# Background work of a fused attention kernel: due steps for the feed-forward products, and two slots a step for one half of the mixing

## The chip, the cores and the metric

The kernel runs on one core of one Trainium2 chip. Its time is the device time of one execution in microseconds (us), the median of 3 runs. The engines are named as the profile names them: PE is the matrix engine, PEld its weight loads, DVE the vector engine, ACT the scalar engine, POOL the GpSimd engine, SP the engine that issues the transfers.

## The reference

Three layers follow each other, all in float32, for 4 batches of 576 positions and a model width of 512:

```python
scores = np.where(causal, -1e9, scale * q @ k.T + np.minimum(bias, 0.0))   # attention, 8 heads of 64
attn = softmax(scores) @ v
h = xt @ U @ V                                   # mixing over positions, rank 32
u = x + h.transpose(0, 2, 1)
x = u + np.maximum(u @ w_ch1, 0.0) @ w_ch2       # feed-forward, 512 -> 2048 -> 512
out = moe2(x)                                    # 4 single-head causal attentions, the top 2 gated and summed
```

## The kernel before

The program has three stages: the first attention, the rest of the feed-forward, and the second attention. Every float32 product that must be exact is split: an operand is held as a rounded high part and a low part, and one product becomes three (high by high, high by low, low by high). The change touches the first stage alone.

**The first attention.** `Attn.run` (L449) walks over steps. A step computes one tile of the scores of one head (`qk`, L361 and L362, PE), its mask and maximum (`peak`, L372, DVE), and the exponential of the tile before (L379, ACT). Ten steps later (`LAG`) the tile is transposed (`t`, L402 and L405, PE) and copied out of PSUM into `pt` (L85 on ACT, L87 on DVE). There are 5 tiles a head, 2 heads a pair, 4 pairs a batch and 4 batches: 160 steps with scores and some 12 more in which the last tiles drain. So ten steps make a pair, and each step has one `qk` tile, by which steps can be counted in the trace. Every tenth step or so the products with V (`pv`, L429, PE) of a finished pair run, and `pv_done` (L791) copies them into `uT` on ACT (L85).

At the end of every step `fillers(i)` (L913) issues what else the step carries: the operands of coming pairs (`prep_steps`, with DMAs on SP's queue), one or two pieces of the conversion of the weights (`CONVS`, two a step in steps 41 to 69), and as many calls of `background()` (L867) as `BG = (1, 1, 0, 2, 1)` has for the step modulo 5. Everything is issued in the order in which this Python code runs, and each engine works through its own share in that order.

**Background work.** Two queues feed `background()`.

- `mixq` holds the mixing of one batch in two halves (`mix_tasks`, L224). A half is ten tasks: three `rows` (transposes `mx` on PE, then `xh` on ACT and `xl` on DVE), an empty one, `down` (ten products `mt` on PE, then `tt` on ACT and DVE), an empty one, and four `up` (two products `mo` on PE each, then an addition into `uT` on DVE). Half one is queued by `pv_done` of a batch's second pair, half two by that of its fourth. The `up` tasks of half two also split the input of the first feed-forward chunk (`u_split`, L272: `uh` on ACT, `ul` on DVE or POOL); two more tasks follow, the last of which fills the other queue.
- `ffnq` holds the feed-forward of the batch over the first three of the sixteen weight blocks (`ffn_tasks`, L280), for two chunks of 288 positions: per chunk three `first` tasks (twelve products `hps` on PE, then `hh` on ACT and `hl` on DVE) and four `second` tasks (nine products `facc` on PE, then an addition into `stage` on DVE). 14 tasks a batch, for batches 0 to 2. A task whose weights aren't converted yet has to wait; the third block is whole from step 73 on.

The tasks of half two from the first `up` on but the last `KD + 2` may not start while `ffnq` holds anything. `background()` as it was alternates between the queues by a counter, `turn`, as long as both have something that may run. PSUM banks for all these (`bank`, L809) come from the pool of four that the score tiles use, but for one step in ten.

Two more things are issued by step number: `halves` at steps 152, 154, 156 and 158 (weights of the next stage), and `ufirst` at steps 161 to 164, which first empties `ffnq` and then splits the first input of the next stage.

Of the kernel before, what the change touches and what calls it, by code (L numbers as in the profile page):

```python
# [20 lines left out]
DM, DFF, E, R = 512, 2048, 4, 32  # L21
P = 128
NP = H // 2
NT = 5
KD = DM // P
# [27 lines left out]
STREAM = (((0, 0), (3, -3)), ((-1, 4),), ((0, 1),), ((0, 2), (1, -2)), ((1, -1),), ((0, 3),))  # L53
FAST = (40, 70)
RAWS = 4

ENGA = ('vaaaaa', 'aavaav')
ULA = ("vvvv", "gvgg")
# [13 lines left out]
BG = (1, 1, 0, 2, 1)  # L72
# [10 lines left out]
def cp(nc, eng, out, in_):  # L83
    if eng == "a":
        nc.scalar.activation(out=out, in_=in_, func=AF.Copy)  # L85
    else:
        nc.vector.tensor_copy(out=out, in_=in_)  # L87
# [57 lines left out]
def f32_stream(jobs, order):  # L145

    n = len(jobs)
    for i in range(-3, n + 1):
        for pieces in order:
            l = [jobs[i + d][3][x] if x >= 0 else jobs[i + d][x + 3] for d, x in pieces if 0 <= i + d < n]  # L150
            if l:
                def step(l=l):
                    for f in l:
                        f()
                yield step
# [3 lines left out]
def fused_kernel(ctx, tc, qk, v, s, u, vv, w12, wp, out):  # L159
# [17 lines left out]
    full = {}  # L177

    def wjobs(f, width, cpool, wpool, room, fixed={}, raws=2, wide=1):


        def job(c0):
            x, c = divmod(c0, DM)

            def load(raw):
                nc.sync.dma_start(out=raw, in_=w12[f, :, x, c:c + width])

            if f in Wf:
                return f32_stages(nc, cpool, room, load, P, width, f"w{f}_{c0}",
                                  dest=lambda: Wf[f][:, x, c:c + width], fixed=fixed, raws=raws, wide=wide)  # L190

            def use(t):
                if c0 == 0:
                    Wh[f] = wpool().tile([P, 2, DM], F32R, tag="wh", name=f"wh_{f}")
                    Wl[f] = wpool().tile([P, 2, DM], F32R, tag="wl", name=f"wl_{f}")
                wh, wl = Wh[f][:, x, c:c + width], Wl[f][:, x, c:c + width]
                nc.scalar.activation(out=wh, in_=t, func=AF.Copy)  # L197
                yield
                eng = nc.vector if WLE == "v" else nc.gpsimd
                eng.tensor_tensor(out=wl, in0=t, in1=wh.bitcast(F32), op=OP.subtract)  # L200
                full[f] = full.get(f, 0) + width

            return f32_stages(nc, cpool, room, load, P, width, f"w{f}_{c0}", use, fixed=fixed, raws=raws, wide=wide)

        return [job(c0) for c0 in range(0, 2 * DM, width)]
# [478 lines left out]
    with ExitStack() as cx:  # L684
# [5 lines left out]
        NPR = B * NP  # L690
# [8 lines left out]
        def load_v(p):  # L699
            b, pr = divmod(p, NP)  # L700
            Vs[p] = d2.tile([P, NT, P], F32, tag="V", name=f"V_{p}")
            nc.sync.dma_start(out=Vs[p], in_=v[b, pr])
# [88 lines left out]
        def pv_done(p, ps, half=None):  # L791
            b, pr = divmod(p, NP)
            if half is None:
                cp(nc, "a", uT[:, pr, b * S:b * S + S].rearrange("p (a b) -> p a b", a=2), ps)
            else:
                cp(nc, "a", uT[:, pr, b * S + HALF * half:b * S + HALF * half + HALF], ps)
            if half == 0:
                return
            if pr == 1:
                mixes[b] = mix_tasks(b, bank)  # L800
                mixq.extend((f, False) for f in mixes[b][0])
            if pr == NP - 1 and b < B - 1:
                first, then = ffn_a(b)
                m = mixes[b][1]
                for k in range(KD):
                    m[k - KD] = lambda f=m[k - KD], g=first[k]: (f(), g())
                mixq.extend((f, x >= len(m) - KD) for x, f in enumerate(m + [lambda: None, lambda: ffnq.extend(then)]))

        def bank(name):  # L809
            if now[0] in WIDE:  # L810
                return psq.tile([P, 2, 512], F32, tag="qk2", name=name, bufs=1)[:, 0, :]
            return psq.tile([P, 1, 512], F32, tag="qk1", name=name, bufs=4)[:, 0, :]

        now = [0]

        def ffn_a(b):


            def done(c, d, ps):
                if d == 0:  # L820
                    stage["t"] = d2.tile([P, KD, CH], F32, tag="stage", name=f"stage_{c}", bufs=1)
                nc.vector.tensor_tensor(out=stage["t"][:, d, :], in0=ps, in1=uT[:, d, c * CH:c * CH + CH], op=OP.add)
                if d == KD - 1:
                    nc.sync.dma_start(out=aD[:, :, c * CH:c * CH + CH], in_=stage["t"])

            return ffn_tasks(range(FA), [2 * b, 2 * b + 1], d2, bank, done)

        mixq, ffnq, stage, mixes = [], [], {}, {}
# [16 lines left out]
        def use_v(t, x):  # L845
            cs = slice(THIRD * x, THIRD * x + THIRD)
            nc.scalar.activation(out=V4[:, 0, cs], in_=t, func=AF.Copy)
            yield
            nc.vector.tensor_tensor(out=V4[:, 1, cs], in0=t, in1=V4[:, 0, cs].bitcast(F32), op=OP.subtract)

        def job(load, n, name, use):
            return f32_stages(nc, cv, PIECE, load, P, n, name, use, fixed=fixed, raws=RAWS, wide=2)

        jobs = [job(lambda raw: nc.sync.dma_start(out=raw, in_=u), NT * R, "u", use_u)]
        for x in range(S // THIRD):
            jobs.append(job(lambda raw, x=x: nc.sync.dma_start(out=raw, in_=vv[x]), THIRD, f"v{x}",
                            lambda t, x=x: use_v(t, x)))
        jobs += [j for f in range(FA + GROUPS[0]) for j in wjobs(f, PIECE, cv, lambda: w01p, PIECE, fixed, RAWS, 2)]
        convs = list(f32_stream(jobs, STREAM))
# [7 lines left out]
        def background():  # L867


            turn[0] += 1  # L870
            ffn = ffnq and full.get(ffnq[0][0]) == 2 * DM
            if mixq and (turn[0] % 2 or not ffn) and not (mixq[0][1] and ffnq):
                mixq.pop(0)[0]()
            elif ffn:
                ffnq.pop(0)[1]()

        def halves(i):

# [4 lines left out]
            nc.scalar.activation(out=Wh[f][:, x], in_=Wf[f][:, x], func=AF.Copy)  # L883
            nc.vector.tensor_tensor(out=Wl[f][:, x], in0=Wf[f][:, x], in1=Wh[f][:, x].bitcast(F32), op=OP.subtract)

        turn = [0]
        todo = {}
        for i in range(2 * GROUPS[0]):
            todo.setdefault(HALVES + 2 * i, []).append(lambda i=i: halves(i))
# [22 lines left out]

        def fillers(i):  # L913
            p, r = divmod(i, 10)
            now[0] = i % (2 * NT)
            if r == 6 and p < NPR:
                load_v(p)
            if i < 4:
                for _ in range(2):
                    if preps:  # L920
                        preps.pop(0)()
            for x in todo.pop(i, ()):
                x()
            for _ in range(CONVS[FAST[0] < i < FAST[1]][i % NT]):
                if i >= 4 and convs:
                    convs.pop(0)()
            for _ in range(BG[i % NT]):
                background()

        attn.run(pair_ready, pv_done, heads, fillers)  # L930
        for f in convs:
            f()
        while mixq or ffnq:
            background()

# [38 lines left out]
    with ExitStack() as cx:  # L974
# [74 lines left out]
        mixq = mix_tasks(B - 1, bank)[1]  # L1049
# [54 lines left out]
    with ExitStack() as cx:  # L1104
# [185 lines left out]
        for n in range(B * E):  # L1290
            b, e = divmod(n, E)
# [105 lines left out]
```

## Time and profile before

| | before |
|---|---|
| median of 3 runs | 843.0 us (842.58 to 843.82) |
| the profiled execution | 842.4 us, of which 840.6 us is the span from the first to the last instruction |
| granted PE clock | 1.00 over the whole span |
| PE busy | 799.4 us (95%) |
| PEld, DVE, ACT, POOL busy | 740.3, 526.0, 473.8, 322.0 us |
| the chain that ended last | PE 79%, DVE 10%, ACT 5%, DMA 3% |
| first attention | from 9.6 us to 288.7 us of the span |

The profile covers one execution, 0.6 us faster than the median of the runs. Busy time of PE is not the whole story of PE: products are pipelined, so a product shown as 0.30 us long lets the next one start after 0.13 us, and a gap in the row is shorter than the delay that it stands for. The delay is read from the starts.

### The profile page before, as it was taken

The numbers are of one execution on the slowest core, as the hardware profiler recorded it, in microseconds if no ns is written. First come the engines' busy times: TensorE is split into PE (matmuls) and PEld (weight loads), VectorE is DVE, ScalarE is ACT, GpSimd is POOL, SyncE is SP. The second block draws the span as 40 slices with busy tenths as digits, with TensorE's granted clock in tenths as the row PEclk, the third lists the DMA queues.
The fourth block names the chain that finished last, engine by engine and source line by source line (L and its number), as shares of the span: only waits on it lengthen the run. The fifth ranks groups of instructions, "written<-read, shape, count | busy, mean of one in ns | idle before, by whom it ended". The sixth has DMA issues, their size and how long they took to land.

```text
span 840.6 us, 17207 instructions
## 1 busy us (share of the span) xinstructions
PE 799.4 (95%) x6028; PEld 740.3 (88%) x6028; DVE 526.0 (63%) x1559; ACT 473.8 (56%) x1406; POOL 322.0 (38%) x483
## 2 busy tenths in 40 slices
PE   3889999999999899999999999999999989999997
PEld 2767779889888799999999999999999989898875
DVE  7779987776775357646554764455456775756541
ACT  5779996666776444434444442443334566655662
POOL 5647664453452334223322432232343043322231
PEclk9999999999999999999999999999999999999999
DMA  7887785745741342112111221210000111111221
GB/s 212 216 228 191 212 219 159 202 127 144 190 117 44 106 146 61 51 27 51 51 51 34 69 64 38 52 39 26 1 1 9 36 33 40 48 52 39 76 66 62
DMA packets 37048, 75.44 MB, mean 90 GB/s; under 512 B 4712, under 2 KB 8296, under 8 KB 36932
## 3 DMA queue, kind: packets, MB, share of 16 engines
q1 hardware_dynamic: 36964, 74.36, 32.5%
q8 instruction: 48, 0.79, 0.4%
q14 instruction: 36, 0.29, 0.1%
HBM read 38.93 MB, written 8.55 MB: 56 GB/s over the span
## 4 chain that ended last, share of the span: by engine, by line
PE 79%; DVE 10%; ACT 5%; DMA 3%; issue 2%; SPq 0%; POOL 0%; ACTq 0%; POOLq 0%; DVEq 0%
PE hps L1010 21%; PE facc L1028 21%; PE pv L429 4%; PE qkp L1237 4%; PE facc L307 3%; PE pv L589 3%; PE ops L1264 3%; PE hps L293 3%; PE t L402 3%; PE t L560 2%; PE vps L1171 2%; PE qk L361 2%; PE qk L362 2%; PE t L405 1%; DVE P L372 1%
## 5 line engine op out<-in xcount | busy, mean ns | idle before, releaser
L277 POOL TENSOR_TENSOR ul<-uT,uh 128x288 fp32r<-128x288 f32 x117 | 94.5, 828 | 163.9 <-ACT uh L276 138.1
L1015 DVE SCALAR_TENSOR_TENSOR hl<-hps,hh 128x288 fp32r<-128x288 f32 x110 | 50.3, 457 | 150.1 <-ACT hh L1014 150.1
L390 POOL TENSOR_SCALAR P<-P,stat 64x64 f32<-64x64 f32 (+4 forms) x160 | 101.7, 651 | 104.3 <-DVE stat L385 44.6
L1014 ACT ACTIVATE hh<-hps 128x288 fp32r<-128x288 f32 x110 | 45.0, 409 | 147.9 <-PE hps L1010 147.7
L85 ACT ACTIVATE pt<-t 64x64 f32<-64x64 f32 (+5 forms) x272 | 89.5, 358 | 42.0 <-PE t L405 29.6
L1010 PE MATMUL hps<-uh,wl 128*128 128x288 f32 x376 | 111.2, 296 | 0.0
L1010 PE MATMUL hps<-ul,wh 128*128 128x288 f32 x376 | 111.1, 296 | 0.0
L1028 PE MATMUL facc<-hh,wh 128*128 128x288 f32 x376 | 111.1, 296 | 0.0
L1010 PE MATMUL hps<-uh,wh 128*128 128x288 f32 x376 | 111.0, 295 | 0.0
L1028 PE MATMUL facc<-hh,wl 128*128 128x288 f32 x376 | 110.9, 295 | 0.0
L1028 PE MATMUL facc<-hl,wh 128*128 128x288 f32 x376 | 110.8, 295 | 0.0
L379 ACT ACTIVATE P<-P,stat 64x64 f32<-64x64 f32 (+4 forms) x160 | 89.2, 558 | 23.2 <-DVE stat L372 21.2
L548 POOL TENSOR_SCALAR P<-P,stat,pt 128x128 f32<-128x128 f32 (+4 forms) x72 | 45.8, 653 | 118.1 <-DVE stat L543 54.1
L372 DVE CUSTOM_DVE_ANT_0 P<-qk,mask 64x64 f32<-64x64 f32 (+4 forms) x160 | 77.4, 484 | 13.7 <-PE t L405 8.7
L361 PE MATMUL qk<-R,L 128*128 128x64 f32 (+2 forms) x192 | 66.3, 349 | 18.3 <-DVE L L750 9.6
L200 POOL TENSOR_TENSOR wl<-c_a_w,wh 128x256 fp32r<-128x256 f32 x56 | 43.8, 784 | 73.2 <-ACT wh L197 70.6
L1010 PEld LDWEIGHTS hps<-uh,wl 128*128 128x128 f32 x376 | 70.9, 189 | 0.0
L1028 PEld LDWEIGHTS facc<-hh,wl 128*128 128x128 f32 x376 | 70.9, 188 | 0.0
L1010 PEld LDWEIGHTS hps<-ul,wh 128*128 128x128 f32 x376 | 70.8, 188 | 0.0
L1028 PEld LDWEIGHTS facc<-hl,wh 128*128 128x128 f32 x376 | 70.8, 188 | 0.0
L1028 PEld LDWEIGHTS facc<-hh,wh 128*128 128x128 f32 x376 | 70.6, 188 | 0.1
L1010 PEld LDWEIGHTS hps<-uh,wh 128*128 128x128 f32 x376 | 70.6, 188 | 0.0
(211 smaller groups left out, 2230.0 us busy)
## 6 DMA issues: line engine op xcount, KB each, us to landing
c_raw_w<-in_w_dram SPq DMA_DIRECT2D x64, 256.0 KB
uT<-in_qk_dram SPq DMA_DIRECT2D x15, 576.0 KB
L<-HI SPq DMA_DIRECT2D x28, 288.0 KB
V<-in_v_dram SPq DMA_DIRECT2D x16, 320.0 KB
R<-HI SPq DMA_DIRECT2D x14, 288.0 KB
R<-uT SPq DMA_DIRECT2D x14, 288.0 KB
L<-uT SPq DMA_DIRECT2D x14, 288.0 KB
aD<-stage SPq DMA_DIRECT2D x6, 576.0 KB
```

What stands on the lines that cost most here:

```text
L85: nc.scalar.activation(out=out, in_=in_, func=AF.Copy)
L200: eng.tensor_tensor(out=wl, in0=t, in1=wh.bitcast(F32), op=OP.subtract)
L277: eng.tensor_tensor(out=l_, in0=src, in1=h_.bitcast(F32), op=OP.subtract)
L361: nc.tensor.matmul(ps[:, bk, :w], lhsT=q1[:, rows], rhs=k1[:, c0:c0 + w], start=True, stop=False)
L372: nc.vector.tensor_tensor_reduce(out=po, in0=view, in1=mk, scale=-self.scale, scalar=3.0e38, op0=OP.add, op1=OP.min, accum_out=stat[P - M: ...
L379: nc.scalar.activation(out=po, in_=po, func=AF.Exp, scale=-1.0, bias=stat[P - M:, 0, t:t + 1], accum_out=stat[P - M:, 1, t:t + 1])
L390: nc.gpsimd.tensor_scalar(out=pv, in0=pv, scalar1=stat[r0:, 2, t:t + 1], scalar2=1.0 if gate is None else gate(t)[r0:], op0=OP.mult, op1=O ...
L548: nc.gpsimd.tensor_scalar(out=po, in0=po, scalar1=stat[:, 2, s:s + 1], scalar2=1.0 if gate is None else gate(t), op0=OP.mult, op1=OP.mult)
L1010: nc.tensor.matmul(ps, lhsT=w[:, 0, cs], rhs=x, start=i == 0, stop=i == 11)
L1014: nc.scalar.activation(out=hh, in_=ps, func=AF.Relu)
L1015: nc.vector.scalar_tensor_tensor(out=hl, in0=ps, scalar=0.0, in1=hh.bitcast(F32), op0=OP.max, op1=OP.subtract)
L1028: nc.tensor.matmul(accs[c][d], lhsT=w[:, 1, cs], rhs=x, start=f == fs[0] and i == 0, stop=f == fs[-1] and i == 2)
```

## The change

`background()` no longer alternates. Each feed-forward task carries the step from which it is due: task k of batch b is due `PACE[b] * k` steps after the batch's tasks were queued, so three steps apart for batch 0, 2.6 for batch 1, and at once for batch 2. A task that is due and whose weights are there runs before any mixing; otherwise the next mixing task runs. In steps 52 to 57 every step has two slots, whatever `BG` says.

```diff
+RUSH = (52, 58)
+PACE = (3, 2.6, 0)
...
-                mixq.extend((f, x >= len(m) - KD) for x, f in enumerate(m + [lambda: None, lambda: ffnq.extend(then)]))
+                mixq.extend((f, x >= len(m) - KD) for x, f in enumerate(m + [lambda: None, lambda: queue(b, then)]))
+
+        def queue(b, tasks):
+            ffnq.extend((f, g, step[0] + PACE[b] * k) for k, (f, g) in enumerate(tasks))
...
-            turn[0] += 1
-            ffn = ffnq and full.get(ffnq[0][0]) == 2 * DM
-            if mixq and (turn[0] % 2 or not ffn) and not (mixq[0][1] and ffnq):
+            ffn = ffnq and full.get(ffnq[0][0]) == 2 * DM and ffnq[0][2] <= step[0]
+            if ffn:
+                ffnq.pop(0)[1]()
+            elif mixq and not (mixq[0][1] and ffnq):
                 mixq.pop(0)[0]()
-            elif ffn:
-                ffnq.pop(0)[1]()
...
-            for _ in range(BG[i % NT]):
+            for _ in range(2 if RUSH[0] <= i < RUSH[1] else BG[i % NT]):
                 background()
```

The same tasks run, in other steps (a task's steps are counted from the program):

| task | steps before | steps now |
|---|---|---|
| mixing of batch 0, half two | 53 to 61 | 52 to 56 |
| feed-forward of batch 0: first two products | 64, 65 | 58, 60 |
| its other twelve | 73 to 95, every other slot | 73 to 76 (five), 78 to 96 |
| mixing of batch 1, half one | 73 to 90 | 78 to 91 |
| mixing of batch 1, half two | 93 to 103 | 93 to 103 |
| feed-forward of batch 1 | 106 to 128 | 106 to 139 |
| mixing of batch 2, half one | 113 to 129 | 113 to 128 |
| mixing of batch 2, half two | 133 to 141 | 133 to 144 |
| feed-forward of batch 2 | 144 to 161 | 148 to 160 |
| mixing of batch 3, half one | 153 to 165 | 161 to 170 |

The order on DVE around the four `up` additions of batch 0's half two (into `uT` from `mo`) and the four `ul` behind them; before, the piece of steps 58 and 59:

```order
L372 ISA P_116,stat_112<-qk_3_1246,mask 128x448
L372 ISA stat_112 128x1
L262 TENSOR_TENSOR uT<-mo_2_0_1267,uT 128x288
L277 TENSOR_TENSOR ul_0_1272<-uT,uh_0_1271 128x288
L372 ISA P_116,stat_112<-qk_4_1275,mask 128x576
L372 ISA stat_112 128x1
L122 SCALAR_TENSOR_TENSOR pt_105<-pt_106,c_r_w_0_1264 128x256
L262 TENSOR_TENSOR uT<-mo_3_0_1292,uT 128x288
L277 TENSOR_TENSOR ul_1_1297<-uT,uh_1_1296 128x288
```

And now, in steps 55 and 56:

```order
L264 TENSOR_TENSOR uT<-mo_2_0_1206,uT 128x288
L279 TENSOR_TENSOR ul_0_1211<-uT,uh_0_1210 128x288
L264 TENSOR_TENSOR uT<-mo_3_0_1214,uT 128x288
L279 TENSOR_TENSOR ul_1_1219<-uT,uh_1_1218 128x288
L374 ISA P_116,stat_112<-qk_1_1222,mask 128x192
L374 ISA stat_112 128x1
L386 TENSOR_SCALAR stat_110<-stat_110 128x5
L387 RECIPROCAL stat_110<-stat_110 128x5
L124 SCALAR_TENSOR_TENSOR pt_105<-pt_107,c_r_w_768_1203 128x256
L264 TENSOR_TENSOR uT<-mo_2_1_1246,uT 128x288
L279 TENSOR_TENSOR ul_2_1251<-uT,uh_2_1250 128x288
```

An addition and a `ul` stood alone between two maxima (L372) before; now two of each follow each other, twice, so that the eight instructions lie in two steps instead of four. (Line numbers of the changed kernel are 2 higher here.)

The order on PE in step 93, the step in which `pv_done` ends a batch and queues half two of the mixing; before (the first two of nine `facc` rows are shown):

```order
L361 MATMUL qk_3_2167<-R_1_127,L_1_125 128x448
L362 MATMUL qk_3_2167<-HI,L_1_128 128x448
L402 MATMUL t_3_2170<-ident,P_114 128x128 x4
L236 MATMUL mx_1_0_2180<-ident,uT 128x128 x4
L307 MATMUL facc_2_2189<-hh_0_1930,wh_730 128x288
L307 MATMUL facc_2_2189<-hl_0_1931,wh_730 128x288
```

And now (the nine `facc` rows stand between `t` and `mx`; the last of them is shown):

```order
L363 MATMUL qk_3_2167<-R_1_127,L_1_125 128x448
L364 MATMUL qk_3_2167<-HI,L_1_128 128x448
L404 MATMUL t_3_2170<-ident,P_114 128x128 x4
L309 MATMUL facc_2_2180<-hh_0_1802,wh_730 128x288
...
L309 MATMUL facc_2_2180<-hh_2_1982,wl_1402 128x288
L238 MATMUL mx_1_0_2191<-ident,uT 128x128 x4
```

The transposes of the mixing have moved behind a feed-forward product. The same holds in step 113; in step 153 two feed-forward products now stand in the place of the transposes.

The order on PE at the end of the stage, from step 161 on, behind the last `pv` but one; before (the 18 `facc` rows of two tasks come first, of which the last two are shown):

```order
L307 MATMUL facc_3_3928<-hl_2_3776,wh_1359 128x288
L307 MATMUL facc_3_3928<-hh_2_3775,wl_1360 128x288
L402 MATMUL t_2_3944<-ident,P_114 128x128 x3
L405 MATMUL t_2_3944<-ident,P_114 64x128
L402 MATMUL t_3_3956<-ident,P_114 128x128 x4
L259 MATMUL mo_0_0_3966<-V_81,tt_0_3884 128x288 x2
L259 MATMUL mo_1_0_3970<-V_81,tt_0_3884 128x288 x2
L405 MATMUL t_4_3974<-ident,P_114 64x128
L259 MATMUL mo_0_1_3981<-V_81,tt_0_3884 128x288 x2
```

And now:

```order
L238 MATMUL mx_0_0_3905<-ident,uT 128x128 x4
L404 MATMUL t_2_3914<-ident,P_114 128x128 x3
L407 MATMUL t_2_3914<-ident,P_114 64x128
L404 MATMUL t_3_3926<-ident,P_114 128x128 x4
L238 MATMUL mx_0_1_3936<-ident,uT 128x128 x4
L238 MATMUL mx_0_2_3945<-ident,uT 64x128 x2
L407 MATMUL t_4_3952<-ident,P_114 64x128
L404 MATMUL t_0_3959<-ident,P_116 128x128
L407 MATMUL t_0_3959<-ident,P_116 64x128 x2
L250 MATMUL mt_0_3965<-xh_0_0_3910,U_80 128x256
```

The 18 `facc` products have moved to before the `pv`, and all ten tasks of a mixing half now lie among the last transposes, where before only its four `up` tasks lay.

## Rows read from the trace of the kernel before

**Rows 1.** Page of the kernel before: busy time, share, instructions.

```profile
PE 799.4 (95%) x6028; PEld 740.3 (88%) x6028; DVE 526.0 (63%) x1559; ACT 473.8 (56%) x1406; POOL 322.0 (38%) x483
```

**Rows 2.** By stretches: length; busy PE, PEld, DVE, ACT, POOL; clock; DMA share; GB/s.

```profile
81.20:89.40 8.20, 7.46 (x57) 6.51 (x54) 7.64 (x24) 7.80 (x26) 4.72 (x6) 1.00 0.96 240
89.40:114.10 24.70, 23.40 (x179) 17.84 (x177) 22.79 (x73) 22.52 (x76) 16.63 (x25) 1.00 0.69 194
114.10:146.50 32.40, 32.14 (x253) 29.43 (x252) 24.60 (x79) 24.77 (x81) 18.72 (x28) 1.00 0.72 192
146.50:170.60 24.10, 23.79 (x202) 20.63 (x201) 19.73 (x65) 17.68 (x59) 10.95 (x17) 1.00 0.72 186
170.60:217.40 46.80, 45.79 (x370) 42.16 (x368) 32.09 (x107) 31.77 (x104) 19.83 (x34) 1.00 0.54 150
217.40:231.70 14.30, 13.76 (x112) 11.29 (x111) 10.20 (x36) 10.57 (x35) 7.27 (x12) 1.00 0.70 186
231.70:246.30 14.60, 14.17 (x118) 12.52 (x116) 10.31 (x37) 10.89 (x37) 6.29 (x10) 1.00 0.59 153
246.30:273.60 27.30, 26.57 (x214) 24.48 (x211) 17.74 (x55) 18.36 (x56) 10.02 (x16) 1.00 0.11 35
273.60:288.70 15.10, 13.35 (x118) 10.29 (x117) 4.71 (x14) 6.35 (x21) 4.93 (x8) 1.00 0.12 40
```

**Rows 3.** Timeline of PE, steps 93, 113, 133, 153: start, length, line, operation, [idle before].

```profile
152.48 0.60 PE L402 MATMUL t<-ident,P 128*128 128x128 f32 x4
152.92 0.27 PE L236 MATMUL mx<-ident,uT 128*128 128x128 f32 x1
153.45 0.55 PE L236 MATMUL mx<-ident,uT 128*128 128x128 f32 x3 [0.26 <-ACT uT L85]
...
189.22 0.55 PE L236 MATMUL mx<-ident,uT 128*128 128x128 f32 x3 [0.26 <-ACT uT L85]
...
223.66 0.77 PE L236 MATMUL mx<-ident,uT 128*128 128x128 f32 x5 [0.26 <-ACT uT L85]
...
259.99 0.27 PE L236 MATMUL mx<-ident,uT 128*128 128x128 f32 x1
260.72 0.55 PE L236 MATMUL mx<-ident,uT 128*128 128x128 f32 x3 [0.46 <-ACT uT L85]
```

**Rows 4.** Timeline of PE at the end of the stage, from step 163 on.

```profile
280.91 0.51 PE L259 MATMUL mo<-V,tt 128*128 128x288 f32 x2
282.20 0.30 PE L402 MATMUL t<-ident,P 128*128 128x128 f32 x1 [0.78 <-ACT pt L85]
...
282.47 0.51 PE L259 MATMUL mo<-V,tt 128*128 128x288 f32 x2
282.82 0.38 PE L402 MATMUL t<-ident,P 128*128 128x128 f32 x2
```

**Rows 5.** Evictions of the mixing's transposes: duration ns min/median/max, first and last start.

```profile
L85 ACT ACTIVATE xh<-mx x18: 362/586/599, 84.7 to 268.2; 128x512 fp32r<-128x512 f32 x12, 64x256 fp32r<-64x256 f32 x6
L240 DVE TENSOR_TENSOR xl<-mx,xh x18: 408/683/693, 85.3 to 268.9; 128x512 fp32r<-128x512 f32 x12, 64x256 fp32r<-64x256 f32 x6
```

**Rows 6.** Groups of DVE in 89.4 to 114.1: busy us, mean ns, idle before.

```profile
L277 DVE TENSOR_TENSOR ul<-uT,uh 128x288 fp32r<-128x288 f32 x4 | 2.1, 522 | 0.0
L262 DVE TENSOR_TENSOR uT<-mo,uT 128x288 f32<-128x288 f32 x4 | 1.8, 448 | 0.0
```

**Rows 7.** Timelines of ACT and PE in steps 52 and 53.

```profile
82.77 0.40 ACT L85 ACTIVATE uT<-pv 128x288 f32<-128x288 f32 x1
...
81.99 0.45 PE L361 MATMUL qk<-R,L 128*128 128x448 f32 x1
```

**Rows 8.** Timelines of DVE and POOL in step 59.

```profile
94.00 0.75 DVE L277 TENSOR_TENSOR ul<-uT,uh 128x288 fp32r<-128x288 f32 x1
96.05 0.44 DVE L277 TENSOR_TENSOR ul<-uT,uh 128x288 fp32r<-128x288 f32 x1
...
93.70 0.73 POOL L200 TENSOR_TENSOR wl<-c_a_w,wh 128x256 fp32r<-128x256 f32 x1
```

More of the change, by code (lines that the diff above doesn't have):

```diff
@@ L812, in bank @@
             return psq.tile([P, 1, 512], F32, tag="qk1", name=name, bufs=4)[:, 0, :]
-        now = [0]
+        now, step = [0], [0]
         def ffn_a(b):
@@ L884, in halves @@
             nc.vector.tensor_tensor(out=Wl[f][:, x], in0=Wf[f][:, x], in1=Wh[f][:, x].bitcast(F32), op=OP.subtract)
-        turn = [0]
         todo = {}
@@ L914, in fillers @@
             p, r = divmod(i, 10)
-            now[0] = i % (2 * NT)
+            now[0], step[0] = i % (2 * NT), i
             if r == 6 and p < NPR:
@@ L932, in fused_kernel @@
             f()
+        step[0] = NPR * 2 * NT * 2
         while mixq or ffnq:
```

## The prediction

> **What bounds the kernel now.** First the page [rows 1]: PE is busy 799.4 us, 95% of the span, so the change can only save PE's gaps. Then where the gaps lie: the busy time by stretches [rows 2]; the clock is granted in full (1.00) in each. I cut them by steps, counting `qk` tiles: 81.2 is the start of step 52, 89.4 of 58, 114.1 of 73, 146.5 of 91, 170.6 of 106, 217.4 of 130, 231.7 of 140, 246.3 of 148; 273.6 is about step 161 and 288.7 the end of the stage. Two regimes are to be seen. Until step 73 three engines are full together: of the 32.9 us from 81.2 to 114.1 PE is busy 30.86, DVE 30.43, ACT 30.32. After it DVE and ACT fall to two thirds or three quarters, and PE sets the pace, with little idle: 0.26, 0.31 and 1.01 us in the three stretches to 217.4, 0.54 and 0.43 in the two of batch 2's second mixing, 0.73 to 273.6, and 1.75 in the drain. The feed-forward stage behind it starts when the drain ends, so what the first attention gains or loses is taken to arrive at the end.
>
> Shown idle is less than what a wait costs. In step 93 the second transpose of `mx` starts 0.53 us after the first [rows 3]; undisturbed transposes start 0.11 apart (the four of `t` take 0.60 in all, one lasts 0.27: a third of 0.33). The wait cost 0.42 us where 0.26 is shown, 1.6 times as much. I use starts where a row has them, and 1.6 elsewhere.
>
> **The change part by part.** No instruction is added or dropped; PE does the same products. So a moved product costs nothing by itself where PE is full: it takes its 1.2 or 1.6 us in one step instead of another. What counts are the waits in PE's queue, since a product that waits holds everything behind it.
>
> *Transposes right behind a finished batch (steps 93, 113, 153).* `mx` needs `uT`, which ACT is only just copying. The waits are 0.42 in step 93, the same in step 113 (the same 0.26 is shown) and 0.62 in step 153 (0.73 between the starts) [rows 3]. Now a feed-forward product of over 1 us stands ahead in the first two, longer than the wait, and two in the third, with the transposes eight steps later. All three go: −1.46. In step 133 the transposes stay where they are, and so does their wait. Bounds: 0, if another wait of the same length follows at once, and −1.46.
>
> *Feed-forward of batch 1 into steps 130 to 139.* Four `facc` tasks come into the stretch 217.4 to 231.7, which had none. They fill gaps there, but not the wait of step 133. Idle 0.54 less its 0.26 leaves 0.28 shown [rows 2, 3], times 1.6: −0.45. Batch 2's mixing now ends in 231.7 to 246.3 without feed-forward products beside it, so I leave that stretch's 0.43 as it is. Bounds: 0, and −1.1 if that goes too. The stretch 170.6 to 217.4, which gives the work, stays full: ACT and DVE are at 31.8 and 32.1 of 46.8.
>
> *The drain.* Two `facc` tasks leave it; three `rows` and a `down` come in, about the same PE time. The wait of 0.94 us before `t` (1.29 between starts, of which two `mo` take 0.35, as the next two do from 282.47 to 282.82) [rows 4] goes, as PE now has transposes and `mt` to do. But `mt` needs its rows evicted, and little stands between: behind the last `mx` ACT has an `xh` of 0.59 and one of 0.36, then DVE an `xl` of 0.41 [rows 5], together 1.36, while PE has only `t` for about 0.3. New wait 1.06; together +0.12. Bounds: −0.94 if the evictions keep up; +1.8 if `t` waits as before (1.06 alone) and `tt`, priced as the smallest `xh` and `xl` (0.36 + 0.41), is waited for as well.
>
> *Steps 52 to 57.* The mixing of batch 0 ends five steps earlier, and the first two feed-forward products come at 58 and 60. The third still waits for its weights until step 73, so nothing gets ahead over the whole of 52 to 72: the same work in the same 32.9 us. Two costs. The `mx` of step 52 now stand right behind `pv_done`: ACT's copy ends at 83.17, the second transpose would start at 82.10 (the start of step 53's `qk`, 81.99, plus 0.11) [rows 7], a wait of 1.07. And DVE's four additions and four `ul`, 3.9 us [rows 6], move from the second stretch, where DVE has 22.79 of 24.70, into the first, where it has 7.64 of 8.20 [rows 2]. The first then takes 11.5 us or more, 3.3 longer; the second has that work less. I take 0: the sums stay, and PE can run a few tiles ahead of DVE. Bounds: −2.5 (32.9 down to the busiest of DVE and ACT, 30.4) and +4.4 (nothing comes back, and the 1.07 on top).
>
> *Five feed-forward tasks in steps 73 to 76.* They stand together and the mixing follows. PE has 0.26 us of idle in the whole stretch [rows 2]: nothing to gain, and DVE, ACT and POOL have room. 0, bounds ±0.4.
>
> **Sum:** −1.46 − 0.45 + 0.12 = −1.8. The profiled execution took 842.4 us, so 840.6 by it; the median of the runs, 843.0, stands 0.6 higher, so **841.2 us**.
>
> **A rule weighed.** An `ul` of DVE that began while POOL worked on a conversion took 0.75 us, the next, with POOL idle, 0.44 [rows 8]. The Trainium skill, SBUF — State Buffer, section "SBUF: two separate sides", says that DVE instructions with two SBUF inputs and GpSimd share one pair of ports as an exclusive lock, so that the later of the two waits. By that rule the four `ul`, packed into two steps, would each meet a POOL instruction. The row agrees for one of them; whether the others meet one no row can show.
>
> **The rivals.**
> *More comes (0.20).* The 32.9 us of three full engines are uneven inside, and with `hps` earlier they even out by half of the 2.5 bound (−1.25); 217.4 to 246.3 gives its −1.1, and the drain half of its best (−0.5): with −1.46, −4.3, 838.7 us. For it: 1.30 us of idle in 89.4 to 114.1. Against: ACT and DVE are full there, and the same work stays.
> *The waits only move (0.18).* PE works in order and shares four banks with the mixing. Where `mx` no longer waits for `uT`, the following `qk` waits for a bank that `xl` frees, 0.36 to 0.69 us an eviction [rows 5], three times 0.5: the 1.46 comes back, 842.7 to 843.0. Against: with DVE at two thirds evictions aren't late there.
> *Each `ul` waits for POOL (0.06).* 0.31 us longer each, 0.75 less 0.44 [rows 8], on a DVE that is full: 4 x 0.31 = +1.2; 842.4. That is the rule above.
> *Slower: the packed DVE work isn't given back (0.10).* In steps 52 to 57 DVE becomes the bound; every later step's transposes wait for evictions in order, and PE cannot make up in 89.4 to 114.1, where it is busy 23.40 of 24.70. With the 1.07 of step 52 that is +4.4 − 1.8 = +2.6, 845.6 us; it counts as slower while less than 0.9 of the 4.4 comes back. Against: DVE and ACT lose the same work in the second stretch.
>
> **How the numbers follow.** A measurement of this kernel can tell some 0.2%, 1.7 us, from no change, so faster means under 841.3. The forecast has 0.46; its own range is 840.0 to 842.2, and I give 0.28 of it to faster. Faster: 0.28 + 0.20 = 0.48. Slower, over 844.7: 0.10, and 0.03 for a drain at its upper bound beside a lost first term: 0.13. Same: the rest, 0.39. The range of 8 in 10 reaches from 838.3, just beyond the larger gain, to 844.0, which leaves out the slower case and the lowest gains. All bounds together would go from 836.6 to 849.6.
>
> **What would show it.** In the profile after: no wait of `mx` for `uT` in steps 93, 113 and 153, one in 133 and a new one of about 1 us in 52; step 73 starting at 114 us, within 1; the stretch from step 73 to 161 shorter by about 1.9; in the drain a wait of `mt` for `xl` of about 1 us. Step 73 later than 116 us would prove the slower rival, earlier than 113 the larger gain; `qk` waiting for `xl` after step 73, more than 1 us in all, that the waits only moved. I am wrong outright if the time falls by more than 5 us, or if the feed-forward stage changes its length.

## The result

The change made the kernel slower: median 850.03 us over four runs (846.99 to 850.41), against 842.92 us for the kernel before on the same chip; ratio 1.0069, 95% interval 1.0050 to 1.0088. A second set of four runs gave 848.84 us and 1.0072 (1.0055 to 1.0090). The prediction was 841.2 us with a range up to 844.0: wrong in sign and outside its range. One run of e3, of 2691.48 us, is left out of all medians and means below.

The profiled execution took 849.74 us, span 848.0, so 7.4 more than that of before. PE's busy time hardly changed:

```profile
PE 802.8 (95%) x6028; PEld 742.8 (88%) x6028; DVE 524.2 (62%) x1559; ACT 473.9 (56%) x1406; POOL 319.6 (38%) x483
```

The feed-forward stage begins at 296.23 us instead of 288.74: 7.5 us are lost inside the first attention, none behind it. The stretches from step 52 on, cut at the same steps as [rows 2], with the same columns:

```profile
82.24:93.20 10.96, 9.73 (x65) 8.54 (x62) 9.68 (x31) 10.64 (x37) 4.96 (x8) 0.88 0.99 241
93.20:117.10 23.90, 21.77 (x172) 17.14 (x170) 20.90 (x68) 19.96 (x67) 17.27 (x25) 0.98 0.63 179
117.10:150.69 33.59, 33.47 (x260) 30.25 (x258) 24.83 (x81) 24.60 (x80) 17.32 (x27) 1.00 0.68 181
150.69:174.31 23.62, 22.96 (x196) 19.73 (x194) 18.95 (x63) 17.50 (x57) 11.04 (x17) 1.00 0.72 190
174.31:218.20 43.89, 41.62 (x334) 37.47 (x332) 30.58 (x105) 31.12 (x103) 20.54 (x35) 1.00 0.57 159
218.20:236.82 18.62, 17.78 (x144) 15.43 (x143) 11.36 (x38) 11.80 (x39) 6.80 (x13) 1.00 0.49 133
236.82:248.70 11.88, 10.02 (x85) 8.34 (x84) 9.59 (x33) 8.48 (x29) 3.50 (x7) 0.96 0.75 192
248.70:281.00 32.30, 32.30 (x251) 30.57 (x249) 17.48 (x56) 19.23 (x59) 10.44 (x18) 0.96 0.11 34
281.00:296.23 15.23, 12.97 (x117) 9.98 (x116) 5.28 (x14) 7.42 (x22) 5.14 (x8) 1.00 0.12 40
```

Two things are to be seen. PE's idle time grew where feed-forward work was taken away: in steps 106 to 129 from 1.01 to 2.27 us, in steps 140 to 147 from 0.43 to 1.86. And the granted clock, 1.00 in every row of [rows 2], is 0.88, 0.98 and 0.96 in four rows here. Windows of 3 us, same columns, show where it falls, and what PE did before it fell:

```profile
47.00:50.00 3.00, 1.73 (x11) 1.16 (x13) 1.61 (x8) 1.90 (x8) 0.22 (x1) 0.94 0.87 311
50.00:53.00 3.00, 3.00 (x13) 1.47 (x11) 1.99 (x7) 0.75 (x3) 1.69 (x3) 0.50 0.25 56
87.00:90.00 3.00, 2.20 (x13) 1.48 (x13) 2.69 (x11) 2.88 (x12) 0.10 (x1) 1.00 0.97 259
90.00:93.00 3.00, 3.00 (x18) 2.92 (x17) 2.66 (x10) 2.94 (x11) 0.27 (x1) 0.60 1.05 251
244.00:247.00 3.00, 2.10 (x17) 1.68 (x14) 2.88 (x10) 2.43 (x8) 0.00 (x0) 1.00 0.71 173
247.00:250.00 3.00, 2.04 (x8) 1.84 (x9) 2.36 (x12) 2.88 (x12) 1.43 (x4) 0.61 0.64 167
```

Three times the clock stands at 0.5, 1.2 GHz in place of 2.4, each time after a stretch in which PE was busy for 1.73, 2.20 or 2.10 of 3.00 us. The first is over before step 52, where the two programs begin to differ, so it cannot be the doing of the change.

What PE waited for from step 52 to the end of the stage (engine, line, what it waited for: us in total, times, longest):

```profile
PE t L404 <- ACT pt L87: 3.4, 6, 1.0
PE t L404 <- issue: 2.0, 4, 1.2
PE facc L309 <- DVE xl L242: 1.4, 2, 0.8
PE t L404 <- POOL wl L202: 1.3, 1, 1.3
PE hps L1014 <- ACT uT L87: 0.8, 1, 0.8
PE mo L261 <- DVE tt L254: 0.7, 1, 0.7
PE mx L238 <- ACT uT L87: 0.7, 2, 0.4
PE qk L363 <- DVE xl L242: 0.4, 1, 0.4
PE mt L250 <- DVE xl L242: 0.3, 1, 0.3
```

The waits of `mx` in steps 93, 113 and 153 [rows 3] are gone, as predicted; the two that are left are those of steps 52 and 133. Other waits have come or grown: `facc` for a bank that `xl` frees, `mo` for `tt` and `t` for POOL's `wl`, of which before has none from 60 us on, and `t` for `pt` or at issue, 5.4 us where before has 4.0. Places of PE's timeline (the wait for `wl`, in step 67, stands in the table above alone, behind the `qk` at 107.76 us):

```profile
84.22 0.55 PE L238 MATMUL mx<-ident,uT 128*128 128x128 f32 x3 [0.43 <-ACT uT L87]
...
193.38 0.36 PE L363 MATMUL qk<-R,L 128*128 128x192 f32 x1 [0.36 <-DVE xl L242]
...
194.99 0.40 PE L309 MATMUL facc<-hh,wh 128*128 128x288 f32 x1 [0.81 <-DVE xl L242]
...
245.91 0.41 PE L404 MATMUL t<-ident,P 128*128 128x128 f32 x2 [0.63 <-ACT pt L87]
...
247.96 0.87 PE L404 MATMUL t<-ident,P 128*128 128x128 f32 x3 [1.23 <-issue]
```

### The profile page after: what moved, and what is told of

Same layout as the page of the kernel before. It is cut to its first block, busy times and chain, and to the rows that moved or that the text cites. A ratio compares the mean times of both kernels' runs of the same rounds, so it can differ in the third digit from the quotient of the medians.

```text
span 848.0 us, 17216 instructions
## 1 busy us (share of the span) xinstructions
PE 802.8 (95%) x6028; PEld 742.8 (88%) x6028; DVE 524.2 (62%) x1559; ACT 473.9 (56%) x1406; POOL 319.6 (38%) x483
## 4 chain that ended last, share of the span: by engine, by line
PE 82%; DVE 7%; ACT 4%; issue 2%; DMA 2%; POOL 1%; SPq 1%; DVEq 0%; ACTq 0%; POOLq 0%
PE hps L1014 21%; PE facc L1032 21%; PE pv L431 5%; PE qkp L1241 5%; PE t L404 3%; PE hps L295 3%; PE facc L309 3%; PE pv L591 3%; PE ops L1268 3%; PE vps L1175 3%; PE t L562 2%; PE qk L363 2%; PE qk L364 2%; PE t L407 1%; DVE P L374 1%
## 5 line engine op out<-in xcount | busy, mean ns | idle before, releaser
L392 POOL TENSOR_SCALAR P<-P,stat 64x64 f32<-64x64 f32 (+4 forms) x160 | 99.8, 639 | 107.5 <-DVE stat L387 47.6
L404 PE MATMUL t<-ident,P 128*128 128x128 f32 x320 | 60.5, 289 | 11.2 <-ACT pt L87 6.1
```

Of the source, the lines that this page charges most:

```text
L392: nc.gpsimd.tensor_scalar(out=pv, in0=pv, scalar1=stat[r0:, 2, t:t + 1], scalar2=1.0 if gate is None else gate(t)[r0:], op0=OP.mult, op1=O ...
L404: nc.tensor.transpose(ps[:, P * kb:P * kb + P], Pn[:, c0:c0 + P], ident)
```

## The experiments

My theory after this reading was: the loss has one part in the order of the work (feed-forward products taken from places where they had filled PE's waits) and one in the clock. Rivals: the rush alone, or the drain alone, or the due times in proportion to how late they put the products. The change was therefore taken apart: the order in which products and mixing alternate, the feed-forward ahead of the mixing at the end, the due times of each batch, the rush.

| run | what it has of the change | median us (runs) | mean clock | ratio to before, 95% |
|---|---|---|---|---|
| e0 | nothing | 842.9 (10) | 0.9977 | 0.9994 (0.9982 to 1.0007) |
| e1 | order alone | 842.0 (10) | 0.9976 | 0.9993 (0.9979 to 1.0006) |
| e2 | order, rush | 844.3 (10) | 0.9945 | 1.0008 (0.9995 to 1.0022) |
| e8 | order, rush, products held | 842.1 (11) | 0.9983 | 0.9988 (0.9979 to 0.9996) |
| e11 | order, last first | 841.4 (11) | 0.9974 | 0.9978 (0.9966 to 0.9989) |
| e12 | e8 and e11 together | 841.9 (12) | 0.9957 | 0.9986 (0.9972 to 1.0000) |
| e4 | order, due times of batch 0 | 843.5 (10) | 0.9964 | 0.9999 (0.9988 to 1.0009) |
| e5 | e4 and last first | 842.6 (10) | 0.9972 | 0.9992 (0.9980 to 1.0004) |
| e3 | all but the rush | 847.4 (6) | 0.9973 | 1.0040 (1.0025 to 1.0055) |
| e6 | e3, `ul` on POOL | 845.8 (6) | 0.9975 | 1.0037 (1.0023 to 1.0051) |
| e13 | e3, `uh` on POOL | 850.3 (4) | 0.9935 | 1.0079 (1.0054 to 1.0105) |
| e9 | e3, one product moved | 845.9 (6) | 0.9970 | 1.0040 (1.0028 to 1.0052) |
| e10 | e3, batch 1 due 2 apart | 843.6 (10) | 0.9980 | 1.0006 (0.9994 to 1.0018) |
| e7 | all | 848.8 (4) | 0.9945 | 1.0072 (1.0055 to 1.0090) |
| e14 | all, products held | 847.7 (4) | 0.9960 | 1.0052 (1.0032 to 1.0073) |

Runs of one kernel spread by 3 us and more, in part with the clock: among the runs of before those at 1.000 took 840.8 to 843.1 us and the five at 0.992 took 845.1 to 845.9, so some 0.4 us for each 0.001 of mean clock (an estimate; those at 0.998 alone spread from 841.8 to 845.0). The sets of runs stem from several chips, and the mean clock of before went from 0.9968 to 0.9979 among them. The traces are sharper than the medians. From step 48 on, until two programs differ, their steps agree within 0.03 us as long as the clock is full and no transfer is late; the exception here is step 60, where kernels that are the same differ by up to 0.4. From step 73 to step 159 e0, which is the kernel before, drifts by 0.17 against the first trace of before, so a difference of 0.2 or less says nothing. So the second table counts from the start of step 48 (its first `qk` in the timeline), and gives how much later than in before a step starts. No column but the last has a stretch at half clock behind step 48:

| start of step | before | e1 | e11 | e5 | e3 | e7 (change) | change, first profile |
|---|---|---|---|---|---|---|---|
| 58 | 14.94 | 0.00 | -0.01 | 0.00 | 0.00 | +1.97 | +2.77 |
| 66 | 30.10 | +0.36 | +0.28 | +0.08 | +0.09 | -0.32 | +0.86 |
| 73 | 39.67 | +0.33 | +0.26 | +0.09 | +0.11 | +0.76 | +1.94 |
| 103 | 93.27 | +0.07 | -0.02 | +0.81 | +0.82 | +1.51 | +2.69 |
| 143 | 163.01 | -0.32 | -0.42 | +0.35 | +1.55 | +2.25 | +3.41 |
| 148 | 171.80 | -0.31 | -0.42 | +0.35 | -0.80 | -0.10 | +1.41 |
| end | 766.14 | -0.50 | -1.29 | -0.69 | +3.13 | +3.77 | +6.32 |

(At step 148 the last three columns have three `hps` of batch 2 still to do, about 4.8 us, which the others have done.) Neighbouring columns differ by one part. Counted from step 73 on, behind that exception, e1 gains 0.83, e11 1.55, e5 0.78, and e3 and e7 lose 3.02 and 3.01; the rush shows at step 73. At full clock, then: order -0.83, last first -0.72, due times of batch 0 +0.77, due times of batch 1 **+3.80**, rush +0.65: together +3.7. (The other pairs for two of these agree: e1 to e4 gives +0.7 for the due times of batch 0, e4 to e5 -0.6 for last first.) Between the change's two profiles lie 2.55 us more, two stretches at half clock. The third lies ahead of step 48, where the first profile loses 1.0 against before (step 29 starts 0.35 earlier, step 33 1.00 later). In the means over runs the change is some 6 us slower than before; the +3.7, and 1.2 estimated from the mean clocks, leave about 1 us that is not explained here.

### The kernel before, and the order alone

e0 is the kernel before. e1 flips the turn of its alternation: wherever both queues have work, product and mixing change places, and so a feed-forward product comes ahead of `mx` in steps 93, 113 and 153. All else stays:

```diff
-        turn = [0]
+        turn = [1]
```

> The kernel before, unchanged, for its clock over several runs. The profile of the change shows three stretches at a granted clock of 0.5, the first of them (49.67 to 53.08 us) before the two programs differ. If such stretches are chance, some runs of this kernel show a mean clock under 1.000 too and are 1.0 to 1.4 us longer for each 0.002 of it, 842.5 to 846. If they are the doing of the change, every run here is at 1.000 and 842.6 to 843.8.

> Only the turn of the alternation is flipped, so that a feed-forward product stands ahead of the first transposes in steps 93, 113 and 153; no due times, no rush; all else alternates as before. Theory of the prediction: the three waits of 1.46 us go, 841.5. Theory that the waits only move: qk or facc wait for a bank that xl frees, 842.7 to 843.3, or up to 844 if the new waits are longer than the old.

e0: the falls are chance in part. Seven of its ten runs were below 0.999, and its profile has one stretch at half clock, at 36.25 us. The profile of before on which I predicted happened to have none. e1: both theories have a share. The three waits are gone, and from step 73 the trace gains 0.83 us, not 1.46: 0.26 by step 103, 0.39 by step 143 and 0.18 in the rest, where 0.42, 0.42 and 0.62 had been waited for. Behind the same steps stand new waits:

```profile
PE facc L307 <- DVE stage L822: 0.3, 1, 0.3
...
PE qk L361 <- DVE xl L240: 0.3, 1, 0.3
```

A product or a `qk` that comes to the bank too early now waits where `mx` had waited: some 0.6 of the 1.46 moved on. (The flip also changes the order inside steps 73 to 91, 113 to 129 and 153 to 161, so the 0.83 is the worth of the whole flip, not of the three waits alone.)

### The rush

e2 is the kernel before with two slots a step in steps 52 to 57 (its alternation then has the turn of e1). e8 holds the two products that become possible by it to steps 64 and 65, where before has them. e3 takes the rush out of the change; e7 is the change again; e14 is the change with the two products held. The edits of e2 and of e8, the second cut to its line:

```diff
-            for _ in range(BG[i % NT]):
+            for _ in range(2 if 52 <= i < 58 else BG[i % NT]):
...
+            due = max(step[0], 64) if b in ALT else ffnq[0][2] if ffnq else 0
```

> The kernel before with two slots a step in steps 52 to 57 and nothing else; as a consequence its alternation has the same turn as the run with the order alone. Theory that the rush costs by its own waits (xl, tt, POOL) and by the clock after its lull: 2 to 4 us above the run with the order alone, 844 to 847, with a stretch at 0.5 near 90 us. Theory that the rush costs nothing (its lost time comes back by step 73): within 0.8 us of the run with the order alone, 841 to 843.5.

> The rush alone, with the first two feed-forward products of batch 0 held to steps 64 and 65, where the kernel before has them; the rest as in the run with the order alone. Theory that the rush costs because it takes these products out of steps 64 to 67, where PE then waits for the attention's chain (1.1 to 1.3 us in step 67 for POOL) and often falls to half clock: the waits of steps 65 to 67 go, the mean clock is 0.9965 or more and the time within 0.7 us of 842.5 (the run with the order alone). Rival, the rush costs by its own waits in steps 52 to 57 (mx for uT 0.43, mo for tt 0.69 shown): as the rush alone, 843.5 to 844.5 and 0.9945.

> The changed kernel itself, for its mean clock over more runs. If the rush adds stretches at half clock, as it did alone (0.9945 against 0.9976), the mean clock is 0.993 to 0.995, where the change without rush had 0.9973, and the median 849 to 850. If the first profile was unlucky: 0.997 and 847 to 848.

> The whole change (mean of eight runs 849.1, mean clock 0.9945), with the first two products of batch 0 held to steps 64 and 65. Theory that the rush costs because it empties steps 64 to 67: the waits there go, the mean clock is 0.9965 or more, 846.4 to 847.3. Rival, the rush and the due times cost together in another way: 848.3 to 849.5 at 0.9945.

What the rush does by itself is given back: e7 is 1.97 us late at step 58 and 0.32 early at 66. It loses 1.1 us from there to step 73, where the two products of steps 64 and 65 are missing. PE's waits in steps 65 to 67 of e2:

```profile
104.86 0.30 PE L402 MATMUL t<-ident,P 128*128 128x128 f32 x1 [0.45 <-POOL P L390]
105.94 0.41 PE L402 MATMUL t<-ident,P 128*128 128x128 f32 x2 [0.36 <-ACT pt L85]
107.89 0.85 PE L402 MATMUL t<-ident,P 128*128 128x128 f32 x3 [1.12 <-POOL wl L200]
```

And the same stretch in 3 us windows, first e2, then e7:

```profile
105.00:108.00 3.00, 1.52 (x11) 1.14 (x11) 2.90 (x9) 2.81 (x11) 2.14 (x3) 0.99 1.00 227
108.00:111.00 3.00, 3.00 (x12) 2.22 (x14) 2.82 (x10) 2.96 (x12) 2.49 (x5) 0.50 0.91 296
```

```profile
106.00:109.00 3.00, 1.33 (x10) 0.94 (x10) 2.87 (x11) 2.65 (x11) 2.02 (x3) 1.00 0.91 208
109.00:112.00 3.00, 3.00 (x28) 2.30 (x26) 2.63 (x9) 2.96 (x12) 2.71 (x5) 1.00 0.91 281
```

PE is busy half the time while DVE and ACT are full, and behind it the clock falls in e2 (there, not near 90 us as expected), but not in e7, with the same lull. A lull may be followed by a fall or not, so its price is read from the mean over runs: 0.9945 in e2 and in the eight runs of the change, 0.9976 in e1. In e8 all three waits of steps 65 to 67 are gone, step 73 starts 0.57 us earlier than in e1, the mean clock is 0.9983 and the median 2.3 us below e2. The theory held for the time, and the rush's own waits (`mx` 0.4, `mo` 0.7, both still in e8) cost nothing in the end. That the lull of steps 65 to 67 is what lowers the mean clock is not shown: of the three falls in e2's profile two, at 36 and 74 us, lie ahead of step 52, and e12 below has no such lull and a mean clock of 0.9957.

e14 confirms it in part. Its waits in 65 to 67 are gone too, the mean clock rose to 0.9960 and the median fell by 1.2 us, but the time stayed above the expected 846.4 to 847.3, and the intervals of the two ratios overlap. In its trace step 73 starts no earlier than in e7 (0.75 late, against 0.76), since the next thing late took the gain back, a transfer:

```profile
111.77 0.27 PE L363 MATMUL qk<-R,L 128*128 128x64 f32 x1 [0.93 <-DMA L<-uT]
```

### The due times, by batch

e3 is the change without the rush, its due times counted from step 57. In e4 batches 1 and 2 alternate as before, in e5 batch 1 does; e10 sets batch 1's due times 2 steps apart, so that its products end at step 131. First e10's edit, behind the cut two lines of e4 and e5:

```diff
-RUSH = (52, 58)
-PACE = (3, 2.6, 0)
+RUSH = (0, 0)
+PACE = (3, 2, 0)
...
+            if b in ALT and turn[0] % 2 and mixq and not mixq[0][1]:
+                ffn = False
```

> The changed kernel with the rush taken out; the feed-forward due times counted from step 57 as in the change, so that from step 66 on both do the same in every step. Theory that rush and its clock are the larger part of the loss: 845.5 to 847. Theory that the due times are (feed-forward late in batch 1, mixing without feed-forward beside it in steps 140 to 147 and 161 to 170): 848 to 850, and the stretch from step 106 to the end of the first attention still 3 to 4 us longer than before.

> No rush; the due times three steps apart stand for the feed-forward of batch 0 alone, and the products of batches 1 and 2 alternate with the mixing exactly as in the run with the order alone, step by step from step 106 on. Reading of the two profiles at full clock: steps 73 to 103 took 1.0 us longer with the due times, so 843.3 to 843.8. Rival, the due times of batch 0 cost nothing and all lies behind: 842.2 to 842.8.

> As the run with due times in batch 0 alone, and the feed-forward of batch 2 stands ahead of the mixing at its end, so that three rows tasks and a down move into the drain; batch 1 alternates as before. Theory that the loss is made where batch 2's mixing ends alone (steps 143 to 147), which this kernel has at its old place: within 1 us of the run with due times in batch 0 alone, 842.5 to 844.5. Rival, the drain makes the loss: 845.5 or more, with waits of over 2 us behind step 161.

> The change without the rush, batch 1's products due 2 steps apart in place of 2.6, so that they are done at step 131, batch 2's mixing ends at 143 as before and its feed-forward stands in steps 144 to 146 again; in steps 113 to 120 products and mixing alternate. Theory that batch 1's 2.6 costs at two places, xl in steps 115 and 116 and the lull of steps 144 to 147: 842.5 to 844.0. Rival, holding products back costs in proportion, wherever they end: 845 to 846.

e3 lies between its two cases: the larger part of the loss is not the rush's. e4 and e5 came out as expected: in the means the due times of batch 0 cost 0.9 us (0.5 with each set taken against before on its own chip) and the drain gains 0.8. With batch 1's 2.6 added to e5, the time rises by 4.7 us (3.80 in the traces); with 2 in its place (e10) the trace ends level with that of before (0.16 ahead of it, no more than e0 drifts). So holding products back does not cost in proportion; it costs where they leave a place empty. PE's waits of e10 from step 106 to 147 are 0.8 us in all:

```profile
PE qk L363 <- ACT uT L87: 0.3, 1, 0.3
PE mx L238 <- ACT uT L87: 0.3, 1, 0.3
PE mx L238 <- DVE xl L242: 0.2, 1, 0.2
```

Against it stand in e3 the 1.17 us shown for `xl` in steps 115 and 116 and the 1.86 of steps 146 and 147, the places shown above for the change. e10 puts both back, the products between the `mx` and the `hps` into steps 144 to 146.

### The banks of steps 113 to 116

In e3 three pairs of `mx` follow each other in steps 113 to 115, where the alternation had put a product between. e9 moves one product from step 116 to 114:

```diff
-            ffnq.extend((f, g, (step[0], 57)[b == 0] + PACE[b] * k)
+            ffnq.extend((f, g, 114 if (b, k) == (1, 4) else (step[0], 57)[b == 0] + PACE[b] * k)
```

> The change without the rush (mean 847.3), and one feed-forward product of batch 1 is taken from step 116 to step 114, between the second and the third pair of transposes of that half. Theory that three rows tasks in a row fill the banks and facc and qk then wait for xl (1.05 and 0.61 us between starts in steps 115 and 116): both go, 845.3 to 846.2. Rival, the wait only moves to the next bank: 846.9 to 847.7.

The medians fell by 1.5 us, but the ratio to before on the same chip is 1.0040 for both, and the trace shows less: counted from step 73 it ends only 0.48 earlier than e3, and the rest lies ahead, where the two kernels are the same. The waits moved:

```profile
PE mx L238 <- DVE stage L827: 0.5, 1, 0.5
PE t L404 <- ACT pt L87: 0.3, 1, 0.3
PE qk L363 <- DVE xl L242: 0.3, 1, 0.3
```

The rival is nearer. One product in another slot does not undo the queue of evictions; e10, which alternates over the whole half, does.

### The lull of steps 143 to 147

Here batch 2's mixing ends with four `up`, each with a `uT` addition and an `ul` on DVE and a `uh` on ACT, and no feed-forward product stands beside them. e6 moves these four `ul` to POOL, e13 the four `uh` (first e6's line, behind the cut e13's):

```diff
-            uu[c, k] = u_split(fua, c, k, nc.vector if ULA[c % 2][k] == "v" else nc.gpsimd)
+            uu[c, k] = u_split(fua, c, k, nc.vector if ULA[c % 2][k] == "v" and c != 4 else nc.gpsimd)
...
+            cpy.tensor_copy(out=h_, in_=src)
```

> The change without the rush, and the four ul of batch 2's first chunk run on POOL, which is idle in steps 145 to 147, in place of DVE; all else the same. Theory that DVE, full with additions, ul and peaks in steps 143 to 147, delays exp, the evictions and so the transposes t (waits of 0.63 and 1.23 us): most of these 1.9 us goes and the time falls by 1.5 to 2.5, to 844.8 to 845.8. Rival, PE lacks work there whatever DVE does, the attention's chain alone sets the pace: the waits stay within 0.5 us and the time within 0.7 of 847.3.

> The change without the rush (mean 847.3), and the four copies uh of batch 2's first chunk run on POOL in place of ACT; ul stays on DVE. Theory that ACT, busy without a break from 240 to 245 us there with exp, the evictions and these copies, sets PE's pace: PE's waits in steps 143 to 147 (1.86 us shown) fall to 0.6 or less, and the time to 845.3 to 846.2. Rival, the chain peak, exp, normalisation, transpose is as long whatever ACT does beside it: waits over 1.2 us, 846.7 to 847.6.

e6: the shown waits fell from 1.86 to 1.18, and from step 73 the trace by 0.62: a third of what the theory asked, and about what its rival allowed. e13: no gain at all; the `exp` (line 384) now waits for DVE's peaks, and PE waits for 1.60 us. ACT of e13:

```profile
240.22 0.56 ACT L384 ACTIVATE P<-P,stat 128x320 f32<-128x320 f32 x1 [0.53 <-DVE stat L377]
...
243.57 0.78 ACT L384 ACTIVATE P<-P,stat 128x576 f32<-128x576 f32 x1 [1.27 <-DVE stat L377]
```

In e6 ACT works without a break from 240 to 245 us, in e13 DVE does. Both engines are full there, and read together the two runs say that whichever is relieved, the other sets the pace; in e6 POOL has a part in it too, as 0.5 of PE's waits end with an `ul` that it was given. e13's median is worse still beside a lower mean clock (0.9935); its profile has a stretch at half clock from the lull on (and another behind 690 us):

```profile
244.00:247.00 3.00, 2.14 (x9) 1.94 (x10) 2.41 (x12) 2.78 (x12) 1.53 (x4) 0.54 0.61 187
247.00:250.00 3.00, 3.00 (x15) 3.00 (x14) 0.36 (x2) 0.60 (x1) 1.06 (x2) 0.50 0.00 0
```

What does take the lull away is PE work beside it: in e10, with `hps` again in steps 144 to 146, PE is busy 11.65 of the 12 us from 236 to 248, and there is no such wait. That DVE and ACT together, both relieved, would do it as well was not tried.

### A version faster than both

e11 has the two parts that gained, the order and batch 2's feed-forward first. e12 adds the rush with its products held. Of e11's edit:

```diff
-        now, step = [0], [0]
+        now, step, turn = [0], [0], [1]
...
+ALT = (0, 1)
```

> The two parts that gained, together: the order alone (turn of the alternation flipped), and batch 2's feed-forward ahead of the mixing at the end; no rush, no due times. If the gains add up (0.3 to 0.6 and 0.7 against before's 843.1): 841.6 to 842.3, faster than both kernels. Rival, they don't add up: 842.5 or more.

> The order alone and batch 2's feed-forward first, which together had a mean of 841.6, with the rush of steps 52 to 57 and its two products held to steps 64 and 65; no due times otherwise. If the rush so held gains beside them what it gained beside the order alone (0.5 in the trace, 0.6 in the means): 840.9 to 841.3. Rival, it gains nothing more: 841.4 to 842.

The two gains add up: e11 took 841.37 us, ratio 0.9978 (0.9966 to 0.9989), the fastest kernel here. e12 gained nothing more, so its rival holds: its trace waits 0.60 us for the transfer `L<-uT` in step 70, as e14 does, and its mean clock is 0.9957. (e12 and e14 ran on one chip, e8 on another; whether the late transfer belongs to the chip is open.) What the held rush gained in e8 can't be counted on.

## Why the prediction was wrong, point by point

- **Transposes behind a finished batch (-1.46).** The waits went where I said; the gain was 0.83, a little over half of the term. The rest moved on, as the rival "the waits only move" had it, which I had called unlikely because DVE is at two thirds there. A share over a stretch says nothing of the half microsecond behind an eviction.
- **Feed-forward of batch 1 into steps 130 to 139 (-0.45).** This is the step that failed. The working counted what the products fill where they arrive, and for the place they leave it said that the stretch "stays full", and of batch 2's mixing without products beside it, "I leave that stretch's 0.43 as it is". That stretch's idle time became 1.86, and steps 106 to 129 lost 1.3 more, both in shown idle, which is less than the delay. Measured: +3.80 in place of -0.45.
- **The drain (+0.12).** Measured -0.72 (e1 to e11), inside the bounds given. In e11 the wait of `t` went as said; what came is one of 1.04 for `tt` and 0.33 for `stat`. In the change itself a `t` still waits 0.96 and `mt` 0.34 for `xl`.
- **Steps 52 to 57 (0, bounds -2.5 to +4.4).** The packed DVE work was given back as argued: -0.32 at step 66. What failed is "the same work in the same 32.9 us": I had asked what DVE gains and loses, and not what PE is left with in steps 64 to 67. Measured +0.65 at full clock, and about 1.1 more by the clock (an estimate from means over runs: 0.0028 of it, at 0.4 us for 0.001). The sign I named for the slower rival, step 73 later than 116 us, came true (117.10) for other reasons: of its 2.95 us, 1.0 was lost before step 52 and 1.2 by the clock.
- **Five tasks in steps 73 to 76 (0, within 0.4).** Measured +0.77, for all due times of batch 0: in step 96 of the change `facc` waits 0.61 (shown) for `xl` behind three pairs of `mx`, the pattern of step 116.
- **The rule weighed.** In the change the four `ul` behind the rush took 0.45 or 0.46 us each, two of them while POOL worked on `P` and none beside a conversion: that rival did not come. That Vector instructions with two SBUF inputs and GpSimd hold a shared pair of ports in turn (the Trainium skill, SBUF — State Buffer, section "SBUF: two separate sides") does show elsewhere: in e6 an addition of DVE, 0.75 us in e3, took 1.44 beside an `ul` of 0.80 on POOL. Its row starts 0.03 us ahead of POOL's, so which of two near ties waits is not settled by the order of their rows.
- **The clock.** I had read "the clock is granted in full in each" stretch and priced nothing on it. The two stretches at half clock behind step 48 are 2.55 of the 7.4 us between the two profiles, and 1.0 is lost ahead of it, where the third lies.
- **Signs.** The `mx` signs held, the wait of step 52 was 0.43 shown (0.7 by the 1.6 of the prediction) instead of about 1, `qk` waited 0.4 for `xl` where more than 1 would have shown that the waits only moved (`facc` did so for 1.4), and the stretch from step 73 to 161 became longer by 4.4 us, not shorter by 1.9. "Outright wrong if the feed-forward stage changes its length": it did not.

## What to carry to other kernels

A product moved to where it fills a wait is also taken from somewhere: price the place that it leaves, step by step, by what the other engines still have to do there. On this PE, 95% busy, matrix work whose operands were long ready covered the packed work of DVE and ACT, so try first to spread it evenly; alternating it with the mixing did this for nothing. And compare traces from a step where the programs are still the same: there 0.2 us could be told, where medians told about 1.

## What was not expected of the hardware

The granted clock is not a constant of a stretch that is nearly full. After 3 us windows in which PE was busy about half the time it fell to half in some cases and not in others: it fell after 1.52 us of work (e2), 1.73 and 2.10 (the change), and not after 1.33 (e7), 1.77 (e3) and 1.15, in the kernel before:

```profile
47.00:50.00 3.00, 1.15 (x9) 0.80 (x11) 1.31 (x5) 1.80 (x6) 0.00 (x0) 1.00 1.01 335
50.00:53.00 3.00, 3.00 (x27) 1.96 (x24) 2.65 (x11) 1.47 (x6) 2.11 (x3) 1.00 0.13 37
```

One place tells more. At 34 to 35 us, where all the kernels here are the same, PE waits for the transfer `L<-uT`. Of the seven traces in which it waited there for 1.25 to 1.80 us, six have a fall at 36 us; of the ten with a shorter wait, one has (e6, two waits of 0.7). So a part of what looks like chance in the clock begins with a transfer that came late. The longest single wait shown ahead of a fall in the first attention was 1.80 us (e7), and e12 waited 1.68 without one. The Trainium skill, TensorE: Matmul & The Clock Gate, section "HAM oscillation — how this bites in real kernels", says that idle gaps of PE bring the clock back to half. The falls here lie behind idle time too, but in none of these lulls was PE idle throughout. The two falls of the change behind step 48 cost 1.2 and 1.4 us, read against e7. What decides whether a lull is followed by a fall stays open: the same program, step for step, had it in one run and not in the next.
